# The second MLP's output product in seven block products, with its operand sums made by accumulating DMAs

## The chip, the cores and the metric

The kernel runs on one core of one Trainium2 chip. The metric is the device time of one execution in microseconds (us). The kernel before took 588.51 us (median of three runs, 586.87 to 592.11).

## The reference, cut to what matters

A sliding-window attention with sinks gives x (1536 tokens by 512), and two MLPs follow it:

```python
x = attention(q, k, v, n_sink, window)          # 1536 x 512
h = x @ w_in;   x = (h * clip(h + 3, 0, 6) / 6) @ w_out     # MLP1, d_ff = 2048
h = x @ w_in2;  g = h * sigmoid(1.702 * h)                  # MLP2, d_ff = 2048
out = g @ w_out2                                            # 1536 x 512, float32
```

Everything is float32. The change touches the last line alone, and of it two of the three blocks of 512 tokens.

## The kernel before, in words

**Products.** A float32 operand is split into a high part hi (rounded to the type fp32r) and the remainder lo, and a product a·b is three matmuls into one PSUM bank: hi·hi, hi·lo, lo·hi. A matmul loads 128x128 weights (LDWEIGHTS, row PEld of the profile) and streams 512 columns past them. The split of a 512-column tile is one cast on ACT (ScalarE) and one subtraction on DVE (VectorE).

**Stages.** The attention (24 steps) is interleaved with MLP1, whose three token blocks take 16 slices of d_ff (f) each: `up` (line 739, matmuls at L752) and `down` (L780, matmuls at L812). Then comes MLP2. Its middle token block runs alone, slice by slice, up and down. The first and the last block run together in the *pair* stage: for two slices of W_in at a time, `pair` (L585) takes the four quarters of that piece of W_in and of the two token blocks as a 2x2 block matrix product and computes it with seven block products instead of eight (Winograd's form of Strassen's method). Each block product is six matmuls at L628 into one of three banks p, q and s; the products b11, b21, t3, t2, t1, b22, t4 accumulate on those banks in turn, and between two products on the same bank ACT or DVE copies or adds what the bank holds so far (`put`, `add`). The sums of W_in's quarters are made by one DMA copy on the queue of SP, one accumulating DMA issued by POOL (L599) and three DVE instructions.

The gate then gives four quarters of g: two for the first token block, which are split and multiplied by W_out at once (24 matmuls at L812 per pair), and two for the last block, which are kept in spare tiles (`store`). When the eight pairs are through, the *rest* stage (`rest`, L729) multiplies the kept ones by W_out: 16 slices of 12 matmuls at L812, the last two slices quarter by quarter (`last_two`, L790) so that the results leave one after another. So W_out's product takes 2 x 16 x 12 = 384 matmuls of 512 columns for these two blocks.

**What sets the order.** The kernel runs under a hand-made planner (`Plan.issue`, L369). Each step is an `op` with the engines that may run it, a cost in ns, and a due time; `issue` plays the whole program with these costs, picks for the engine that can start soonest the step with the earliest due time, and emits the instructions in that order. On the chip each engine runs its own list in order and waits on semaphores; the DMAs that POOL issues stand in POOL's list, those of SP in SP's. Rings of buffers (`plan.ring`: w0, s, w1, g for split operands, u, aside and spare for float32 tiles, bank for the eight PSUM banks) bound how far a step may run ahead.

## Time and profile before

| what | value |
|---|---|
| runs | 588.51 us median of 3, 586.87 to 592.11 |
| profiled execution | 590.02 us, its span 587.9 us |
| TensorE (PE) busy | 569.3 us, 97% of the span |
| weight loads (PEld) | 492.8 us, beside the matmuls |
| DVE / ACT busy | 435.5 us (74%) / 365.0 us (62%) |
| POOL busy | 8.5 us |
| mean granted TensorE clock | 0.994 of full speed |

The span leaves out what lies before the first and after the last instruction, here 2.1 us. Busy times of PE overlap from one matmul to the next, since the end of a matmul is modelled: the distance from start to start tells how long one takes in a stream. The chain of waits follows the end of the program back from releaser to releaser. A duration on ACT or DVE is likewise longer than the distance to the next instruction on that engine.

### The profile page before, as it was taken

The numbers are of one execution on the slowest core, as the hardware profiler recorded it, in microseconds if no ns is written. First come the engines' busy times: TensorE is split into PE (matmuls) and PEld (weight loads), VectorE is DVE, ScalarE is ACT, GpSimd is POOL, SyncE is SP. The second block draws the span as 40 slices with busy tenths as digits, with TensorE's granted clock in tenths as the row PEclk, the third lists the DMA queues.
The fourth block names the chain that finished last, engine by engine and source line by source line (L and its number), as shares of the span: only waits on it lengthen the run. The fifth ranks groups of instructions, "written<-read, shape, count | busy, mean of one in ns | idle before, by whom it ended". The sixth has DMA issues, their size and how long they took to land.

```text
span 587.9 us, 10650 instructions
## 1 busy us (share of the span) xinstructions
PE 569.3 (97%) x4194; PEld 492.8 (84%) x4194; DVE 435.5 (74%) x912; ACT 365.0 (62%) x751; POOL 8.5 (1%) x18
## 2 busy tenths in 40 slices
PE   7789999999999999999999999999999999999996
PEld 6678877788888888888888888888888888888885
DVE  7799999999995756469999999973455555444542
ACT  6887775974666755465566596544575666455543
POOL 0000000000000000000000000000000100000000
PEclk8999999999999999999999999999999999999999
DMA  8974355145350000001444430510031110001102
GB/s 264 372 232 162 118 196 163 42 148 183 124 205 17 1 2 1 1 0 45 170 144 159 169 120 3 198 32 1 0 90 27 26 20 20 0 1 33 40 1 76
DMA packets 13480, 53.02 MB, mean 90 GB/s; under 512 B 1712, under 2 KB 3760, under 8 KB 9328
## 3 DMA queue, kind: packets, MB, share of 16 engines
q1 hardware_dynamic: 12272, 51.22, 26.0%
q0 software_dynamic: 1152, 1.05, 1.2%
q8 instruction: 35, 0.57, 0.4%
q14 instruction: 21, 0.17, 0.1%
HBM read 47.02 MB, written 3.15 MB: 85 GB/s over the span
## 4 chain that ended last, share of the span: by engine, by line
PE 76%; DVE 8%; ACT 7%; DMA 7%; issue 2%; SPq 0%; ACTq 0%
PE bank L812 37%; PE bank L752 22%; PE bank L628 12%; DMA stage<-in_w_dram 6%; ACT pexp L1011 3%; PE bank L1039 2%; PE bank L988 1%; DVE wf L503 1%; DVE wf L496 1%; ACT pexp L1028 1%; DMA wf<-in_kq_dram 1%; PE bank L1062 1%; ACT pts L445 1%; DVE pexp L1003 1%; ACT wf L475 1%
## 5 line engine op out<-in xcount | busy, mean ns | idle before, releaser
L812 PE MATMUL bank<-wg 128*128 128x512 f32 x1140 | 275.7, 381 | 0.5 <-ACT wg L445 0.3
L812 PEld LDWEIGHTS bank<-wg 128*128 128x128 f32 x1140 | 213.6, 189 | 32.6 <-DVE wg L570 1.3
L752 PE MATMUL bank<-xy,w0h 128*128 128x512 f32 x512 | 154.1, 382 | 1.5 <-DVE xy L1089 1.0
L752 PEld LDWEIGHTS bank<-xy,w0h 128*128 128x128 f32 x512 | 95.5, 189 | 15.3 <-DVE xy L1089 1.3
L752 PE MATMUL bank<-xy,w0l 128*128 128x512 f32 x256 | 97.0, 379 | 0.0
L554 DVE TENSOR_TENSOR wg<-wf,wg 128x512 fp32r<-128x512 f32 x95 | 65.3, 687 | 34.3 <-ACT wg L445 34.3
L445 ACT CAST wg<-wf 128x512 fp32r<-128x512 f32 x89 | 55.0, 618 | 44.7 <-PE bank L812 44.2
L570 DVE TENSOR_TENSOR wg<-u,wg 128x512 fp32r<-128x512 f32 x80 | 54.9, 687 | 13.8 <-ACT wg L445 12.9
L445 ACT CAST wg<-u 128x512 fp32r<-128x512 f32 x75 | 46.5, 620 | 19.7 <-DVE u L769 13.9
L554 DVE TENSOR_TENSOR w0l<-wf,w0h 128x512 fp32r<-128x512 f32 x72 | 49.3, 685 | 12.0 <-ACT w0h L445 11.8
L764 ACT ACTIVATE u<-bank,three 128x512 f32<-128x512 f32 x48 | 32.8, 684 | 40.1 <-PE bank L752 40.0
L752 PEld LDWEIGHTS bank<-xy,w0l 128*128 128x128 f32 x256 | 48.4, 189 | 6.8
L769 DVE SCALAR_TENSOR_TENSOR u<-u,bank 128x512 f32<-128x512 f32 x48 | 32.7, 682 | 25.9 <-ACT u L764 25.8
L1011 ACT ACTIVATE pexp<-pexp,nb 128x196 f32<-128x196 f32 x96 | 43.0, 450 | 8.6 <-DVE nb L1003 8.4
L475 ACT ACTIVATE wf<-stage 128x1024 f32<-128x1024 f32 x32 | 37.8, 1183 | 15.9 <-DMA stage<-in_w_dram 15.0
L445 ACT CAST w0h<-wf 128x512 fp32r<-128x512 f32 x60 | 36.7, 611 | 5.3 <-PE bank L628 4.6
L496 DVE SCALAR_TENSOR_TENSOR wf<-stage,wf 128x1024 int32<-128x1024 int32 x32 | 39.1, 1222 | 0.4
L503 DVE SCALAR_TENSOR_TENSOR wf<-stage,wf 128x1024 int32<-128x1024 int32 x32 | 39.1, 1221 | 0.2
L581 ACT ACTIVATE u<-bank 128x512 f32<-128x512 f32 x32 | 19.1, 596 | 31.1 <-PE bank L752 22.9
L628 PE MATMUL bank<-xy,w0h 128*128 128x512 f32 x128 | 38.1, 379 | 0.0
L1039 PE MATMUL bank<-ident,pexp 128*128 128x128 f32 x192 | 29.5, 296 | 4.1 <-DVE pexp L1030 2.3
L1039 PEld LDWEIGHTS bank<-ident,pexp 128*128 128x128 f32 x192 | 23.7, 151 | 9.3 <-ACT pexp L1028 2.3
(139 smaller groups left out, 630.4 us busy)
## 6 DMA issues: line engine op xcount, KB each, us to landing
stage<-in_w_dram SPq DMA_DIRECT2D x32, 1024.0 KB, 5.0
wf<-in_kq_dram SPq DMA_DIRECT2D x8, 520.0 KB, 11.1
vc<-in_vc_dram SPq DMA_DIRECT2D x12, 320.0 KB, 6.4
vb<-in_v_dram SPq DMA_DIRECT2D x10, 256.0 KB, 6.5
kept<-in_kq_dram SPq DMA_DIRECT2D x4, 520.0 KB, 10.9
out_dram<-stage SPq DMA_DIRECT2D x8, 256.0 KB, 3.0
aside<-wf SPq DMA_DIRECT2D x8, 128.0 KB, 2.0
aside<-wf POOLq DMA_DIRECT2D x8, 128.0 KB, 2.7
```

What stands on the lines that cost most here:

```text
L445: eng.copy(out, in_)
L475: lambda e: e.activation(w.tile.bitcast(F32), top.bitcast(F32), AF.Abs),
L496: lambda e: e.scalar_tensor_tensor(out=w.tile, in0=top, scalar=-0x40000000, in1=w.tile, op0=ALU.bitwise_and, op1=ALU.bitwise_or),
L503: lambda e: e.scalar_tensor_tensor(out=w.tile, in0=low, scalar=29, in1=w.tile, op0=ALU.logical_shift_right, op1=ALU.bitwise_or),
L554: lambda e: e.tensor_tensor(out=lo.tile[at], in0=of(), in1=hi.tile[at].bitcast(F32), op=ALU.subtract),
L570: lambda e: e.tensor_tensor(out=at(gl), in0=parted(u.tile), in1=at(gh).bitcast(F32), op=ALU.subtract),
L628: e.matmul(bank.tile, l, woven(r), start=(begin and j == 0 and k == 0), stop=(j == 1 and k == 2), skip_group_check=True,)
L752: e.matmul(h.tile[:, :n], w, woven(x), start=(c == 0 and k == 0), stop=(c == NC - 1 and k == 2))
L764: lambda e: e.activation(u.tile[:, :n], h.tile[:, :n], AF.Relu, bias=three, scale=1.0),
L812: e.matmul(yb.tile, l, woven(r), start=(begin and k == 0), stop=(end is not None and k == 2))
L1011: lambda e, n=n: e.activation(pes[n].tile[:, :W], pes[n].tile[:, :W], AF.Exp, bias=nbs[n].tile, scale=-1.0, accum_out=z.tile[:, n : n + 1],),
L1039: e.transpose(pt.tile[:, n * P : (n + 1) * P], pes[2 * a + j].tile[:, x * P : (x + 1) * P], ident)
```

## The change

W_out's product for the first and the last token block is now also a 2x2 block product in seven instead of eight: the rows are the two token blocks, the inner index the two slices of a pair (eight pairs), the columns the two halves of W_out's 512. A new function `downs` runs after all eight pairs and replaces `rest`, `last_two` and the 24 matmuls that each pair had. It computes seven products (numbered 0 to 6 below), each over eight pairs; each pair of a product is 12 matmuls of 256 columns (four 128-token quarters, three hi/lo parts). `left` splits a sum of g quarters, `right` a sum of W_out quarters; the signs go into the split. Sums are made in place by accumulating DMAs on POOL's queue (`more`): of W_out, 16 of 256 KB before product 2 and four more for product 3; of g, eight before the products, then eight in each of `after11`, `after12` and `after22`, beside products 0, 1 and 2. There are 52 in all. Two quarters of g now overwrite W_in's columns in their own tiles, two go negated by ACT into spare tiles. The mix of W_in that a DMA pair had made goes to DVE. The results of the two blocks leave in 16 stores of 128 KB. The planner counts 1300 ns of POOL for an issue; the accumulating DMAs' ring grows from 1 KB to 2 KB of each partition, and three mask tiles of together 1 KB become temporary. W_out's columns are laid out differently by the host, and the middle block's four results are put back in order by their copies.

```diff
@@ -425,6 +420,8 @@
                     self.dma_free = max(start + 600, self.dma_free) + cost
                     end = self.dma_free + LAND - 600
                     self.lanes.append(end + 300)
+                elif eng == "POOL":
+                    at[eng] = start + ISSUE
...
-            plan.op(
-                [("SP", 131072 / RATE_DMA)], lambda e: e.dma_start(out=s1(), in_=a21()), None, reads=[w2], writes=[sa],
-                chain="mix",
-            )
-            plan.op(
-                [("POOL", 3000)], lambda e: e.dma_start(out=s1(), in_=a22(), accum_op=ALU.add), None, reads=[w2],
-                writes=[sa], chain="mix",
-            )
             for to, x, y, how, reads, into in (
+                (s1, a21, a22, ALU.add, [w2], sa),
...
                 plan.op(
-                    [("PE", 6 * 216)], mm, due[i] + step[0] * 2037,
...
+                    [("PE", 6 * 216)], mm, due[i] + step[0] * 1296,
+                    reads=[wh, wl] + [b for x in xs for b in x[2]], writes=[bank], chain=("up", i),
...
-            u11, u21, one, low = Buf(cls="u"), Buf(cls="u"), Buf(cls="aside"), Buf(cls="aside")
-            g12, g22 = Buf(cls="spare"), Buf(cls="spare")
+            u11, u21, one, low = (Buf(cls="u") for _ in range(4))
+            n11, n12 = Buf(cls="spare"), Buf(cls="spare")
+            g21, g22 = (Buf(wf[f].bitcast(F32)[:, :512]) for f in (f1, f2))
...
             put(p, one, product(p, wa, 0, "b11", True))
             at = product(q, wa, 256, "b21", True)
             add(one, q, q, at)
             gate(q, u11, at + 600)
+            less(u11, n11, at + 1200)
+            put(p, low, product(p, wb, 256, "t2", False))
             put(s, g22, product(s, wb, 0, "t3", True))
-            at = product(p, wb, 256, "t2", False)
-            put(p, low, at)
-            g[i, 0] = split_g(u11, at)
-            wo[i, 0] = split_of(w1, slice(512, 1024), "w1", 1)
             at = product(p, wc, 0, "t1", False)
             add(g22, p, g22, at)
             gate(g22, g22, at + 1200)
-            at = product(p, wc, 256, "b22", False)
-            gate(p, g12, at)
             at = product(s, wd, 0, "t4", False)
             add(low, s, s, at)
             gate(s, u21, at + 600)
-            g[i, 1] = split_g(u21, at + 1200)
-            wo[i, 1] = split_of(w2, slice(512, 1024), "w1", 1)
-            store[f1], store[f2] = g12, g22
+            less(u21, n12, at + 1200)
+            gate(p, g21, product(p, wc, 256, "b22", False))
+            parts[f1 // 2] = {"11": n11, "12": n12, "21": g21, "22": g22}
+
+        def less(x, to, after):
+            plan.op([("ACT", 478)], lambda e: e.mul(to.tile, x.tile, -1.0), after, reads=[x], writes=[to])
+
+        def downs(t0):
...
+            for n in range(pairs // 2):
+                for k, (j, cols) in enumerate(((0, 0), (0, 256), (1, 0), (1, 256))):
+                    x = Buf(fa[:, 4 * n + j : 4 * n + 4 : 2, 512 + cols : 768 + cols])
...
+                less(b[n, "12"], b[n, "12"], None)
+                less(b[n, "21"], b[n, "21"], None)
+
+            def more(x, to):
+                plan.op(
+                    [("POOL", ADD_DMA)], lambda e: e.dma_start(out=to.tile, in_=x.tile, accum_op=ALU.add), None,
+                    reads=[x], writes=[to],
+                )
...
+            def left(x, sign, cls):
+                hi, lo = Buf(cls=cls + "h"), Buf(cls=cls + "l")
...
+                plan.op(
+                    [("ACT", 520)], lambda e: e.mul(at(hi), parted(x.tile), sign), None, reads=[x], writes=[hi],
+                    chain="split0",
...
+                plan.op(
+                    [("DVE", 602)],
+                    lambda e: e.scalar_tensor_tensor(
+                        out=at(lo), in0=parted(x.tile), scalar=sign, in1=at(hi).bitcast(F32),
+                        op0=ALU.mult, op1=ALU.subtract,
+                    ),
+                    None, reads=[x, hi], writes=[lo],
...
+            def right(x, cls="w1", to=None, after=()):
...
+                plan.op(
+                    [("ACT", 520)], lambda e: copy(e, at(hi), of()), None, reads=[x], writes=[hi], chain="split1",
...
+                plan.op(
+                    [("DVE", 602)],
+                    lambda e: e.tensor_tensor(out=at(lo), in0=of(), in1=at(hi).bitcast(F32), op=ALU.subtract),
...
+            def product(k, a, sign, r, bank, begin, then):
+                share = 4 // len(bank)
...
+                    def mm(e):
+                        at, gh, gl = x
+                        th, tl = (t.tile[:, :, n % 2 * P : (n % 2 + 1) * P] for t in y)
+                        for e4 in which:
+                            to = bank[e4 // share].tile[:, e4 % share * 256 : e4 % share * 256 + 256]
+                            hi, lo = quarter(at(gh), e4), quarter(at(gl), e4)
+                            for m, (l, t) in enumerate(((hi, th), (hi, tl), (lo, th))):
+                                e.matmul(
+                                    to, l, woven(t), start=(begin and n == 0 and m == 0 and e4 % share == 0),
+                                    stop=(n == pairs - 1 and m == 2), skip_group_check=True,
+                                )
...
+                    plan.op(
+                        [("PE", len(which) * 3 * 112)], mm, t0 + k * step + n * step // pairs,
...
+                w = []
+                for n in range(pairs):
+                    cls = ("w0", "s")[n % 2] if k < 2 else ("g", "w0", "s")[n % 3]
+                    if (k, n // 2) not in ready:
+                        ready[k, n // 2] = right(b[n // 2, r])
+                    w.append((left(parts[n][a], sign, cls), ready[k, n // 2]))
+                    then(n)
+                    if share == 2 or n < pairs - 2:
+                        quarters(n, *w[n], range(4))
+                if share == 1:
+                    for e4 in range(4):
+                        for n in range(pairs - 2, pairs):
+                            quarters(n, *w[n], [e4])
+                return t0 + (k + 1) * step
...
+            gone, ready = [x for half in halves(512, 512) for c in range(NC) for x in plan.x[half][c]], {}
+            for n in range(pairs // 2):
+                to = [Buf(home[1][:, :, n, :]) for home in (xyh, xyl)]
+                for x in to:
+                    x.readers = [o for y in gone for o in y.readers]
+                ready[0, n] = right(b[n, "11"], to=to)
+                more(b[n, "12"], b[n, "11"])
+            for n in range(pairs // 2):
+                ready[1, n] = right(b[n, "21"], "w1" if n < 2 else "g", None, [plan.last["g"]])
+                more(b[n, "11"], b[n, "21"])
+                more(b[n, "22"], b[n, "21"])
+                more(b[n, "22"], b[n, "12"])
+            bx, by, bz = ([Buf(cls="bank", kind="d") for _ in range(2)] for _ in range(3))
+            end = NBLK - 1
+            none = lambda n: None
+            for n in range(pairs):
+                more(parts[n]["22"], parts[n]["21"])
+
+            def after11(n):
+                more(parts[n]["21"], parts[n]["11"])
+
+            t1 = product(0, "11", -1.0, "11", bx, True, after11)
+            c11 = keep(bx, "u", 1.0, t1)
+
+            def after12(n):
+                more(parts[n]["11"], parts[n]["12"])
+                if n % 2 == 0:
+                    m = n // 2
+                    two = Buf(cls="aside")
+                    pairs_of = lambda: two.tile.rearrange("p (k n) -> p k n", k=2)
+                    plan.op(
+                        [("SP", 262144 / RATE_DMA)], lambda e: e.dma_start(out=pairs_of(), in_=b[m, "11"].tile), None,
+                        reads=[b[m, "11"]], writes=[two], after=[plan.last["mix"]],
+                    )
+                    plan.op(
+                        [("POOL", ADD_DMA)],
+                        lambda e: e.dma_start(out=pairs_of(), in_=b[m, "22"].tile, accum_op=ALU.add), None,
+                        reads=[b[m, "22"]], writes=[two],
+                    )
+                    b[m, "2"] = two
+
+            t2 = product(1, "12", 1.0, "21", by, True, after12)
+            add(by, c11, t2)
+            send(c11, 0, 0, t2)
+
+            def after22(n):
+                less(parts[n]["22"], parts[n]["22"], None)
+                more(parts[n]["11"], parts[n]["22"])
+
+            t4 = product(2, "22", -1.0, "21", bz, True, after22)
+            c22 = keep(bz, "u", -1.0, t4)
+            t6 = product(3, "11", 1.0, "2", bx, False, none)
+            c21 = keep(bx, "spare", 1.0, t6)
+            t7 = product(4, "22", -1.0, "12", bz, False, none)
+            add(bz, c21, t7)
+            send(c21, end, 0, t7)
+            t5 = product(5, "21", -1.0, "11", bx, False, none)
+            add(bx, c22, t5)
+            add(bz, c22, t5)
+            send(c22, end, 1, t5)
+            u4 = keep(bx, "spare", 1.0, t5)
+            bw = [Buf(cls="bank", kind="d") for _ in range(4)]
+            t3 = product(6, "12", -1.0, "22", bw, True, none)
...
+            for e4 in range(4):
+                plan.op(
+                    [("DVE", 335)],
+                    lambda e, e4=e4: e.tensor_tensor(
+                        out=c12[e4].tile[:, :256], in0=bw[e4].tile[:, :256],
+                        in1=u4[e4 // 2].tile[:, e4 % 2 * 256 : e4 % 2 * 256 + 256], op=ALU.add,
+                    ),
+                    t3, reads=[bw[e4], u4[e4 // 2]], writes=[c12[e4]],
+                )
+            send(c12, 0, 1, t3)
...
-        def rest(i):
-            which, t0, n, f, begin, end = items[i]
...
-        def last_two(i):
-
-            for e4 in range(4):
-                for k in (i - 1, i):
-                    which, t0, n, f, begin, end = items[k]
-                    down_of(g[k], wo[k], which, t0, n, begin, end, [due[k] + 1000] * 4, [e4])
...
+        if late:
+            downs(due[-1] + 9072)
...
                 if b.kind == "q":
-                    return h + used.count("q") < 4
+                    return h + used.count("q") < (4 if "y" in used else 6)
...
-                    t += {"pair": 14256, "rest": 2592}.get(items[n][0], 5184 * (RATE if n < 8 else RATE2 if n < 24 else 1))
+                    t += 9072 if items[n][0] == "pair" else 5184 * (RATE if n < 8 else RATE2 if n < 24 else 1)
...
-    nc = _bacc.Bacc("TRN2", target_bir_lowering=False, num_devices=1, dynamic_dma_scratch_size=1024)
+    nc = _bacc.Bacc("TRN2", target_bir_lowering=False, num_devices=1, dynamic_dma_scratch_size=2048)
...
-        return w.reshape(-1, w.shape[1] // 2, 2).transpose(0, 2, 1).reshape(w.shape)
+        return w.reshape(-1, 2, w.shape[1] // 4, 2).transpose(0, 1, 3, 2).reshape(w.shape)
```

Up to the first product of the pair stage, PE's list is the same in both kernels.

PE, the second pair of the pair stage. Before: `bank_4677`, `bank_4703` and `bank_4691` are p, s and q of that pair, the rows at L812 the matmuls with W_out.

```order
L628 MATMUL bank_4703<-xt_4031,sh_4032 128x512 x2
L628 MATMUL bank_4703<-xt_4031,sl_4034 128x512
...
L628 MATMUL bank_4677<-xt_4031,sh_4032 128x512 x2
L628 MATMUL bank_4677<-xt_4031,sl_4034 128x512
...
L812 MATMUL bank_4725<-wg_206 128x512 x3
L812 MATMUL bank_4731<-wg_206 128x512 x3
L628 MATMUL bank_4677<-xy_85,w0h_4672 128x512 x2
L628 MATMUL bank_4677<-xy_85,w0l_4675 128x512
...
L812 MATMUL bank_4649<-wg_206 128x512 x3
L812 MATMUL bank_4654<-wg_206 128x512 x3
```

PE, the same place now: `bank_4625` is p, `bank_4690` s, and nothing but products of pairs is left.

```order
L616 MATMUL bank_4625<-xt_4013,sh_4014 128x512 x2
L616 MATMUL bank_4625<-xt_4013,sl_4016 128x512
...
L616 MATMUL bank_4690<-xt_4013,sh_4014 128x512 x2
L616 MATMUL bank_4690<-xt_4013,sl_4016 128x512
...
L616 MATMUL bank_4625<-xy_70,w0h_4673 128x512 x2
L616 MATMUL bank_4625<-xy_70,w0l_4686 128x512
...
L616 MATMUL bank_4690<-xt_4013,sh_4015 128x512 x2
L616 MATMUL bank_4690<-xt_4013,sl_4017 128x512
```

Between two products on one bank there is now one product on the other, six matmuls; before, it was six and nine for p at the places shown, and more for s.

PE, the beginning of `downs` and the end of the last pair, as it stands now; `bank_5245` and `bank_5246` hold product 0.

```order
L616 MATMUL bank_5053<-xy_70,w0h_5091 128x512 x2
L616 MATMUL bank_5053<-xy_70,w0l_5094 128x512
L732 MATMUL bank_5245<-xy_70,w0h_5229 128x256 x2
L732 MATMUL bank_5245<-xy_70,w0l_5232 128x256
...
L732 MATMUL bank_5246<-xy_70,w0h_5229 128x256 x2
L732 MATMUL bank_5246<-xy_70,w0l_5232 128x256
```

In all 672 matmuls of 256 columns stand at L732, and none of 512 columns after the last pair.

POOL, the accumulating DMAs of g's sums. Before, POOL's list held eight accumulating DMAs, one for each pair:

```order
L599 DMA aside_3970<-wf1_63 128x256
L599 DMA aside_4537<-wf3_65 128x256
L599 DMA aside_4642<-wf5_67 128x256
L599 DMA aside_4743<-wf7_69 128x256
L599 DMA aside_4841<-wf9_71 128x256
```

Now, from the first of `after11` on; `stage` and `vc`, `vb` are spare tiles, a row into `stage0_60<-wf_62` is of `after11`, one into `wf_62<-stage0_60` of `after22`:

```order
L824 DMA aside_5199<-wf_62 128x2x256
L680 DMA stage0_60<-wf_62 128x512
L680 DMA wf_62<-wf_62 128x2x256
...
L680 DMA vc1_67<-wf_62 128x512
L680 DMA stage0_60<-stage0_60 128x512
L680 DMA stage1_61<-stage0_60 128x512
...
L680 DMA vc2_68<-vb1_64 128x512
L680 DMA wf_62<-stage0_60 128x512 x2
L680 DMA wf_62<-stage1_61 128x512 x2
...
L680 DMA wf_62<-vc1_67 128x512
L680 DMA vc2_68<-vc1_67 128x512
```

From the first `stage0_60<-wf_62` to `wf_62<-vc1_67` there are 26, which run in this order.

## Rows read from the trace of the kernel before

**Rows 1.** The page: busy time of each engine, share of the span, instructions.
```profile
PE 569.3 (97%) x4194; PEld 492.8 (84%) x4194; DVE 435.5 (74%) x912; ACT 365.0 (62%) x751; POOL 8.5 (1%) x18
```

**Rows 2.** Windows from the middle block's end: engines' busy us, clock, DMA share, GB/s.
```profile
core 0: us, PE busy (x) PEld busy (x) DVE busy (x) ACT busy (x) POOL busy (x), PEclk, DMA share, GB/s
395.00:424.60 29.60, 29.60 (x139) 25.92 (x138) 11.20 (x19) 13.51 (x25) 0.00 (x0) 1.00 0.00 1
424.60:480.00 55.40, 55.40 (x258) 48.53 (x257) 32.19 (x60) 35.55 (x66) 3.57 (x5) 1.00 0.17 41
480.00:535.30 55.30, 55.30 (x258) 48.40 (x257) 26.46 (x45) 29.26 (x53) 1.65 (x2) 1.00 0.04 8
535.30:582.70 47.40, 47.40 (x220) 41.20 (x218) 22.69 (x35) 23.63 (x42) 0.00 (x0) 1.00 0.12 32
582.70:587.90 5.20, 0.03 (x1) 0.00 (x0) 0.42 (x1) 0.37 (x1) 0.00 (x0) 1.00 0.48 136
```

**Rows 3.** Chain of waits, 423 to 588: start us, us, what.
```profile
424.74 1.29 PE bank L628 x6
...
535.46 47.28 PE bank L812 x219
...
582.76 0.38 ACT vc L445
...
583.17 0.42 DVE vc L447
```

**Rows 4.** Timeline of PE at 67 us: start us, us, instruction, count.
```profile
67.83 1.93 PE L1039 MATMUL bank<-ident,pexp 128*128 128x128 f32 x16
```

**Rows 5.** One line's instructions, L1039: duration ns min/median/max.
```profile
L1039 PE MATMUL bank<-ident,pexp x192: 272/273/473, 10.9 to 207.3; 128*128 128x128 f32 x192
```

**Rows 6.** Timeline of PEld at 96.7 us, behind a pause of PE.
```profile
96.77 0.30 PEld L752 LDWEIGHTS bank<-xy,w0h 128*128 128x128 f32 x2
```

**Rows 7.** One line's instructions, L752: duration ns min/median/max.
```profile
L752 PEld LDWEIGHTS bank<-xy,w0l x256: 189/189/189, 43.9 to 422.2; 128*128 128x128 f32 x128
```

**Rows 8.** Timeline of ACT in the rest stage.
```profile
538.74 0.62 ACT L445 CAST wg<-wf 128x512 fp32r<-128x512 f32 x1 [0.77 <-PE bank L812]
539.26 0.62 ACT L445 CAST wg<-stage 128x512 fp32r<-128x512 f32 x1
539.78 0.58 ACT L445 COPY stage<-bank 128x512 f32<-128x512 f32 x1
...
543.85 0.59 ACT L445 COPY vc<-bank 128x512 f32<-128x512 f32 x1
544.33 0.63 ACT L445 CAST wg<-wf 128x512 fp32r<-128x512 f32 x1
```

**Rows 9.** Timeline of DVE at 361 to 368 us.
```profile
361.47 0.69 DVE L722 SCALAR_TENSOR_TENSOR xt<-vb,xt 128x512 fp32r<-128x512 f32 x1
362.07 0.68 DVE L722 SCALAR_TENSOR_TENSOR xt<-aside,xt 128x512 fp32r<-128x512 f32 x1
...
366.82 0.42 DVE L609 TENSOR_TENSOR aside<-wf,wf 128x256 f32<-128x256 f32 x1
367.15 0.69 DVE L488 TENSOR_SCALAR wf<-wf 128x1024 int32<-128x1024 int32 x1
```

**Rows 10.** Timeline of the first pair: a product's last matmul, the copy or addition behind it.
```profile
425.65 0.38 PE L628 MATMUL bank<-xy,w0l 128*128 128x512 f32 x1
...
426.07 0.59 ACT L445 COPY aside<-bank 128x512 f32<-128x512 f32 x1 [0.68 <-PE bank L628]
...
428.24 0.38 PE L628 MATMUL bank<-xy,w0l 128*128 128x512 f32 x1
...
428.73 0.70 DVE L646 TENSOR_TENSOR bank<-aside,bank 128x512 f32<-128x512 f32 x1 [1.40 <-PE bank L628]
```

**Rows 11.** One line's instructions, L599: the accumulating DMAs that POOL issues.
```profile
L599 POOL DMA_DIRECT2D aside<-wf x8: 862/868/1020, 350.4 to 493.0; - x8
...
DMA to landing us min/median/max: 2.6/2.7/2.8
```

**Rows 12.** The page: DMA queues (packets, MB, share of 16 engines' span), issues (KB, us to landing).
```profile
q0 software_dynamic: 1152, 1.05, 1.2%
...
out_dram<-stage SPq DMA_DIRECT2D x8, 256.0 KB, 3.0
aside<-wf SPq DMA_DIRECT2D x8, 128.0 KB, 2.0
```

More of the change, by code (lines that the diff above doesn't have):

```diff
@@ L528, in plan_mlps @@
             items += [("pair", 0, 512, f, f == 0, None) for f in range(0, NF, 2)]
-            items += [("rest", (NBLK - 1) * 512, 512, f, f == 0, "y" if f == NF - 1 else None) for f in range(NF)]
         due = item_due(items)
         g, wo, ys = {}, {}, {}
-        sums, sixth, extra, store = {}, {}, {}, {}
+        sums, sixth, extra, parts = {}, {}, {}, {}
         def split(i, part):
@@ L727, in scaled @@
             )
-        def rest(i):
-            which, t0, n, f, begin, end = items[i]
-            g[i] = split_g(store[f], None, cls="s" if f == NF - 1 else "g")
-            if f < NF - 1:
-                wo[i] = split(i, 1)
-            else:
-                for k, b in enumerate(extra["t2", 0]):
-                    b.later = lambda k=k: late()["x"](2 * k)
-                wo[i] = split_of(plan.wf[f], slice(512, 1024), None, 1, True, extra["t2", 0])
         def up(i):
@@ L781, in down, with down_of @@
             which, t0, n, f, begin, end = items[i]
[L782 to L797 removed]
+            if which != "pair":
+                down_of(g.pop(i), wo.pop(i), which, t0, n, begin, end, [due[i] + DOWN] * 4)
+        def down_of(gs, ws, which, t0, n, begin, end, at):
             (gh, gl), (wh, wl) = gs, ws
@@ L800, in down_of @@
                 ys["b"] = [Buf(cls="bank", kind="y") for _ in range(4)]
-            for e4 in parts:
+            for e4 in range(4):
                 yb = ys["b"][e4]
@@ L855, in result @@
                 o = Buf(cls="spare" if late else "u")
-                if which == "rest" and e4 == 3:
-                    for x, opt in enumerate(([("ACT", 300)], [("DVE", 335)])):
-                        cols = slice(256 * x, 256 * (x + 1))
-                        plan.op(
-                            opt, lambda e, cols=cols: copy(e, o.tile[:, cols], yb.tile[:, cols]),
-                            when, reads=[yb], adds=[o],
-                        )
-                else:
-                    plan.op(
-                        [("ACT", 478), ("DVE", 602)], lambda e: copy(e, o.tile, yb.tile), when, reads=[yb], writes=[o]
-                    )
+                plan.op(
+                    [("ACT", 478), ("DVE", 602)],
+                    lambda e: copy(
+                        e, o.tile.rearrange("p (h n a) -> p h n a", h=2, a=2),
+                        yb.tile.rearrange("p (a n h) -> p h n a", h=2, a=2),
+                    ),
+                    when, reads=[yb], writes=[o],
+                )
                 rows = out[t0 : t0 + 512, :].rearrange("(l q h) d -> q h l d", l=8, q=4)[e4]
@@ L883, in plan_mlps @@
                     plan_load_w(plan, w2, f + nst - NF, None)
-            {"pair": pair, "rest": rest}.get(items[i][0], up)(i)
-            if i and (i < len(items) - 1 or items[i][0] != "rest"):
+            (pair if items[i][0] == "pair" else up)(i)
+            if i:
                 down(i - 1)
```

110 lines of the change are left out of this document (75 added, 35 removed).

## The prediction, as it was made before the changed kernel ran

> **What bounds the kernel now.** I read the busy times first: PE is busy for 97% of the span [rows 1]. That share alone could hide waits, so I went to windows by stage. From 395 us to 582.7 us PE is busy for all of every window, at a granted clock of 1.00, the 2.4 GHz level, while DVE and ACT are busy for 38% to 64% [rows 2]. The chain of waits says the same: from 424.74 us, where the pair stage begins, it runs over PE to 582.74 us, then through 0.38 us of ACT, 0.42 us of DVE and a store [rows 3]. So in the part that the change touches, time is the number of matmuls times the distance between two of them. That distance is 47.28/219 = 0.2159 us for 512 columns [rows 3]. The stage holds 336 matmuls of pair products and 384 with W_out, with 12 left of the middle block: 732 x 0.2159 = 158.0 us, and the chain has 582.74 - 424.74 = 158.0 us. Nothing else is in it.
>
> **The change, part by part.** The order of instructions ahead of the pair stage is the same, so nothing is won or lost there. The pair products keep their number and width.
>
> *Matmuls with W_out.* 384 matmuls of 512 columns go, 384 x 0.2159 = 82.9 us. In come 7 products x 8 pairs x 12 = 672 matmuls of 256 columns. No matmul of this width and type is in the trace. Half the columns cannot take less than half of 0.2159, 0.108 us, and should not take more than the whole 0.2159; in the same stream lies one weight load per matmul, so the question is whether a load of 128x128 fits into half the time. The nearest row: 16 transposes, each with its own 128x128 float32 load, take 1.93 us together; without the 0.27 us of the last one [rows 5] that is 1.66/15 = 0.110 us from start to start [rows 4]. For the type used here, two loads behind a pause of PE end 0.30 us after the first began; one lasts 0.189 us [rows 7], so the second began 0.11 us after the first [rows 6]. Both rows say that loads can follow at 0.11 us. I take 0.110: 672 x 0.110 = 73.9 us, a gain of **9.0 us** (10.3 at 0.108; at 0.2159 a loss of 62.2).
>
> The Trainium skill has a rule that speaks against this (TensorE: Matmul & The Clock Gate, Part 3, "The mechanism"): a weight load overlaps a running matmul only if it goes to another row group. All matmuls here use all 128 rows. The 512-column stream disagrees with it: load and stream would not fit into 0.2159 us one behind the other. It is a rival below.
>
> *ACT and DVE as possible bounds.* From start to start ACT takes 0.52 us for a cast and 0.48 for a copy from PSUM [rows 8], DVE 0.60 for 512 columns and 0.33 for 256 [rows 9]. In the new pair stage, 8 x 42 x 0.2159 = 72.5 us of PE, the changed order gives ACT 108 wide and 7 narrow instructions, at most 115 x 0.52 = 60 us, and DVE 52 wide and 35 narrow, 43 us. In `downs` ACT has 97, 50 us, DVE 85 wide and 4 narrow, 52 us, against 73.9 us. Neither becomes the bound by its total, and so the splits that the change adds (56 of g's sums, 28 of W_out's) cost nothing as long as they arrive in time. Without that cover each would cost the 0.52 + 0.60 us of its chain.
>
> *Turnarounds in the pair stage.* With the W_out matmuls gone, a bank is needed again after one other product, 6 x 0.2159 = 1.295 us. A copy by ACT ends at 426.66, that is 0.79 us after the last matmul gave way (425.65 + 0.216); an addition by DVE ends at 429.43, 0.97 us after 428.46 [rows 10]. So 0.50 and 0.33 us are left. Even in the old order one such gap of six matmuls, behind a copy, stood without a wait of PE [rows 2]. An instruction just begun on the engine holds the copy up by at most 0.52, the addition by 0.60 us. Of four turnarounds in each of eight pairs three go through ACT and one through DVE: 24 x 0.02 + 8 x 0.27 = 2.6 us if that always happens, 0 if never, 24 x 0.54 + 8 x 0.87 = 19.9 us if two instructions stand ahead each time. I take **1.5 us**, since DVE is busy about 60% of the time and mostly with one. In `downs` each pair's operands go ACT, DVE, PE, with four to six buffers; I take **1 us** for the change-over between stages (0 to 9: one pair's 12 x 0.110 = 1.3 us at each of seven products).
>
> *The end.* Before, ACT and DVE copied the two halves of the last bank one after the other; now one DVE addition of 256 columns follows the last matmul, so 0.4 us go [rows 3]. The last store is 128 KB, not 256. From 583.59 us to the span's end the old one took 4.3 us; a landing is 3.0 us for 256 KB to DRAM and 2.0 for 128 KB within the chip's memory [rows 12], so it gains between 0 and 1.0; I take 0.4. Together **0.8 us** (0.4 to 1.4).
>
> *POOL's sums.* The eight old accumulating DMAs took 0.87 us of POOL to issue and landed after 2.7 us [rows 11]; they moved 128 KB each, and 1.2% of 16 x 587.9 us over 8 is 14.1 us of one engine, 0.88 us of all sixteen [rows 12]. The new ones move 256 KB: between 0.88 us, were it all cost per packet, and 1.76 us, were it all bytes. The W_out sums have the 72.5 us of the pair stage. Product 3 reads g's sums of `after11`, product 4 those of `after22`, so 26 DMAs may run from the first split of product 0 (about 1 us before it starts) until product 4 wants its last pair (4 x 10.56 + 7 x 1.32 = 51.5 us after that start, less 1.5 us for the split). With 2.7 us for the last to land they stay hidden up to 48.3/26 = 1.86 us each. The upper end, 1.76, just fits: I charge nothing, and what is late if it does not fit is product 4. The larger ring and the moved mask tiles are charged nothing: POOL sends at most one DMA per 0.87 us, and the masks are made in the first microseconds, which the lists leave as they were. The strided copies of the middle block's four results run beside matmuls.
>
> *Sum*, against the profiled execution of 590.02 us: -9.0 + 1.5 + 1.0 - 0.8 = -7.3, 582.7 us. That execution lay 1.5 us above the median of the runs, so for the median **581.2 us**.
>
> **Rivals.**
> *The gain stays, but PE waits for copies and splits* in most turnarounds: 4 to 11 us of waits in place of 2.5. For it: the cover of 24 matmuls per pair is gone and the lists are fixed in advance. Against it: the loads of ACT and DVE. Time 582.7 to 589.7.
> *The sums of g come late* and product 4 waits: slower than before. The place is POOL's list from the first `stage<-wf` on, the price 26 x (r - 1.86) us for r us per DMA; it eats the whole gain at r = 2.14 and makes the kernel 1% slower at 2.37. At r = 2.5 it costs 16.6 us: 598 us. For it: the upper bound of r lies close to 1.86, and no row shows such DMAs back to back. Against it: fewer, larger packets cost less per byte. The Trainium skill's line for such DMAs (DMA: Bandwidth & Descriptors, "Anatomy of one DMA"), 2.0 us and bytes/436e3, would add an estimated 0.6 us for 256 KB each and keep them hidden; the trace's 2.7 us for 128 KB is above its 2.3.
> *Loads and matmuls run in turn*, 0.11 + 0.110 us each: 672 x 0.22 = 147.8 us, 73.9 more, 655 us. Against it stand [rows 3, 4].
> That the change does not do what it says is excluded by the lists: 672 matmuls of 256 columns stand there.
>
> **How the numbers follow.** A measurement here tells about 1%, 5.9 us, from no change, so faster means below 582.6. The forecast (waits up to 3.9 us) gets 0.52, and 576.8 to 582.6 us: at the low end -10.3 - 1.4 without any wait. The waits rival gets 0.25, of which 0.01 by the runs' scatter still counts as faster; the late sums get 0.13, of which 0.04 within 1%; the loads in turn 0.04; 0.06 what I have not named, spread evenly. Faster 0.55, same 0.30, slower 0.15. The range 576.8 to 592 holds the forecast, the waits and the mild half of the late sums, 0.8.
>
> **What would show it.** 672 matmuls at 0.110 us from start to start, with loads beside them, show the main term; 0.2 would refute it. Waits of PE in the pair stage on ACT copies or DVE additions above 3 us in all show the first rival. POOL's DMAs in `downs` more than 1.9 us apart, and PE, ACT or DVE waiting for them in product 3 or 4, show the second. From the last matmul to the end there should be 4.4 us. I am wrong if the pair stage is longer than 76 us or `downs` longer than 77.

## The result, and the profile after

The changed kernel takes 582.45 us (median of six runs, 581.77 to 584.52) where the kernel before took 590.38 us on the same chip (median of six): a ratio of 0.9879, 95% interval 0.9845 to 0.9914, so 1.2% faster and more than the 1% that the prediction set as the bound. Forecast were 581.2 us and a gain of 7.3; measured is a gain of 7.9 (5.1 to 9.2).

The profiled execution of the change took 584.52 us, the slowest of the six, with a span of 582.6. The page's busy times, which answer to [rows 1]:

```profile
PE 563.2 (97%) x4482; PEld 496.6 (85%) x4482; DVE 456.8 (78%) x951; ACT 389.4 (67%) x803; POOL 54.2 (9%) x62
```

The chain of waits, start us, us, what, which answers to [rows 3]:

```profile
426.10 1.29 PE bank L616 x6
427.39 2.59 PE bank L980 x12
429.98 71.92 PE bank L616 x330
501.89 75.05 PE bank L732 x672
576.95 0.02 issue
576.97 0.42 DVE vb L855
```

The chain still lies on PE from the start of the pair stage to the last matmul. The pair stage takes 501.89 - 426.10 = 75.79 us; its 348 matmuls (12 of the middle block among them) at 0.2159 us are 75.13, so waits can be 0.66 us at most; the trace lists no wait of PE from here to the last matmul. `downs` takes 75.05 us for 672 matmuls, 0.1117 us each, with no piece of another engine between. Together 150.84 us in place of 158.0, a gain of 7.2. Windows of the two stages, columns as in [rows 2]:

```profile
426.10:501.90 75.80, 75.80 (x350) 65.37 (x350) 48.06 (x91) 61.73 (x121) 27.45 (x24) 1.00 0.61 107
501.90:577.00 75.10, 75.03 (x672) 74.84 (x671) 53.95 (x86) 51.21 (x93) 25.30 (x28) 1.00 0.72 127
```

In `downs` the weight loads (third column) are now as busy as PE, 74.84 of 75.10 us; in [rows 2] they were 41.20 of 47.40. ACT is busy for 61.73 and 51.21 us, DVE for 48.06 and 53.95: below PE in both, and 2 to 12% above the 60 and 50, 43 and 52 us worked out.

The end grew. From the last matmul's end, 576.94 us, to the span's end, 582.6, are 5.65 us; before it was 587.9 - 582.74 = 5.16. In the two profiles the pair stage also begins 1.36 us later (426.10 after 424.74); with 0.2 us less outside the span this makes up the 5.5 us between them: 7.2 - 0.5 - 1.4 + 0.2.

### The profile page after: what moved, and what is told of

Read it like the earlier page. It is cut to its first block, busy times and chain, and to the rows that moved or that the text cites. A ratio compares the mean times of both kernels' runs of the same rounds, so it can differ in the third digit from the quotient of the medians.

```text
span 582.6 us, 11436 instructions
## 1 busy us (share of the span) xinstructions
PE 563.2 (97%) x4482; PEld 496.6 (85%) x4482; DVE 456.8 (78%) x951; ACT 389.4 (67%) x803; POOL 54.2 (9%) x62
## 3 DMA queue, kind: packets, MB, share of 16 engines
q0 software_dynamic: 10048, 13.63, 14.8%
## 4 chain that ended last, share of the span: by engine, by line
PE 80%; DVE 9%; ACT 4%; DMA 3%; issue 1%; DVEq 0%; SPq 0%
PE bank L980 24%; PE bank L932 24%; PE bank L732 13%; PE bank L616 13%; DMA stage<-in_w_dram 3%; PE bank L1203 2%; ACT pexp L1175 2%; PE bank L1152 2%; PE bank L1226 2%; DVE wf L500 1%; DVE wf L493 1%; PE bank L1234 1%; DVE pexp L1167 1%; DVE wg L550 1%; DVE wf L485 1%
## 5 line engine op out<-in xcount | busy, mean ns | idle before, releaser
L980 PE MATMUL bank<-wg 128*128 128x512 f32 x768 | 190.0, 382 | 2.7 <-ACT wg L442 2.5
L980 PEld LDWEIGHTS bank<-wg 128*128 128x128 f32 x768 | 143.3, 189 | 24.7 <-ACT wg L442 3.2
L680 POOL DMA_DIRECT2D wf<-wf x24 | 29.0, 1287 | 469.2 <-ACT wf L661 433.9
L442 ACT CAST wg<-wf 128x512 fp32r<-128x512 f32 x78 | 48.2, 618 | 31.9 <-PE bank L980 24.4
L550 DVE TENSOR_TENSOR wg<-wf,wg 128x512 fp32r<-128x512 f32 x64 | 43.9, 685 | 15.3 <-ACT wg L442 15.3
L442 ACT CAST wg<-u 128x512 fp32r<-128x512 f32 x59 | 36.6, 620 | 14.3 <-DVE u L949 14.3
L565 DVE TENSOR_TENSOR wg<-u,wg 128x512 fp32r<-128x512 f32 x64 | 43.9, 685 | 0.9
## 6 DMA issues: line engine op xcount, KB each, us to landing
wf<-in_kq_dram SPq DMA_DIRECT2D x8, 520.0 KB, 11.8
```

What stands on the lines that cost most here:

```text
L442: eng.copy(out, in_)
L550: lambda e: e.tensor_tensor(out=lo.tile[at], in0=of(), in1=hi.tile[at].bitcast(F32), op=ALU.subtract),
L565: lambda e: e.tensor_tensor(out=gl.tile, in0=parted(u.tile), in1=gh.tile.bitcast(F32), op=ALU.subtract),
L980: e.matmul(yb.tile, l, woven(r), start=(begin and k == 0), stop=(end is not None and k == 2))
```

## Experiments

Each ratio is against the kernel before on the same chip. The difference to the changed kernel is (ratio / 0.9879 - 1) x 582.45 us; with both intervals it is known to 3 or 4 us. e2, e12 and e6 leave out part of the sums and serve for times alone.

| run | median, us | ratio, 95% interval | to the change, us |
|---|---|---|---|
| e1_halves (of before) | 593.56 | 1.0057, 1.0032 to 1.0082 | |
| e2_narrow | 583.83 | 0.9884, 0.9830 to 0.9937 | +0.3 |
| e12_narrow2 | 580.72 | 0.9842, 0.9800 to 0.9884 | -2.2 |
| e3_oldchain | 592.51 | 1.0050, 1.0027 to 1.0073 | +10.1 |
| e10_chain | 582.01 | 0.9874, 0.9841 to 0.9907 | -0.3 |
| e6_nosums | 583.42 | 0.9869, 0.9832 to 0.9907 | -0.6 |
| e4_dma8 | 593.87 | 1.0079, 1.0053 to 1.0105 | +11.8 |
| e5_dma8b | 587.33 | 0.9959, 0.9931 to 0.9986 | +4.7 |
| e8_ring1k | 601.32 | 1.0155, 1.0098 to 1.0211 | +16.3 |
| e9_late | 595.72 | 1.0112, 1.0064 to 1.0160 | +13.7 |
| e11_noissue | 593.63 | 1.0081, 1.0039 to 1.0122 | +11.9 |
| e7_tail | 582.50 | 0.9858, 0.9823 to 0.9893 | -1.2 |

### What a matmul of 256 columns costs

**e1_halves.** The kernel before, W_out's matmuls of the two blocks in halves:

```diff
-e.matmul(yb.tile, l, woven(r), ...)
+for j in range(2):    # pair and rest stage
+    e.matmul(yb.tile[:, j * 256 : (j + 1) * 256], l, woven(r[:, :, j * P : (j + 1) * P]), ...)
```

> The kernel before, with each of the 384 matmuls with W_out of the first and the last token block done as two of 256 columns (768 in place of 384); nothing else is changed. If a 256-column matmul always costs the 0.1117 us of the changed kernel's stream (75.05/672): 768 x 0.1117 = 85.8 us for 82.9, so +2.9 us. If 0.110, the prediction's value, were right and the rest of the 75.05 us were small waits: +1.6 us. If half the columns cost half the time (0.108): 0. If the weight loads cost more where the operands lie otherwise: above +5 us.

It is slower by 0.57%, 3.4 us (1.9 to 4.8), where 2.9 were expected. The chain's last long piece, in the rest stage of this run:

```profile
535.75 48.92 PE bank L815 x438
```

48.92/438 = 0.1117 us: the cost goes with the width, in the old place and order too, and is no wait of `downs`.

**e2_narrow, e12_narrow2.** Product 5 streams half the columns; the second run also halves its weights' columns:

```diff
-to, l, woven(t), ...
+to[:, : 2 * few], l, woven(t[:, :, :few]), ...             # e2: few = 64 for product 5, else 128
+to[:few, : 2 * few], l[:, :few], woven(t[:, :, :few]), ...  # e12
```

> The changed kernel, with product 5 streaming 128 of each 256 columns (half of that product's sums are left out). If the weight load sets the 0.1117 us, the distance stays at 0.11 and product 5 takes its 10.7 us as before: the time of the changed kernel, 582.5 us. If the columns set it (256/2.4 GHz and 5 ns), the distance falls to 0.058 inside a group of 12 matmuls, and product 5 shrinks until ACT (16 casts of 0.52 us) or DVE (16 of 0.60 us) bounds it at about 8.3 to 9.6 us: 1 to 2.5 us less.

> As the run with 128 columns streamed in product 5, and with weights of 64 columns in place of 128 there (three quarters of that product's sums are left out). If the load's time goes with the weights' columns, the distance between matmuls falls to about 0.06 us; if it goes with the rows (128, as before) or is fixed, it stays at 0.11 us.

The chain of e2, and then PE's timeline of e12 (start us, us, instruction, count) around the beginning of product 5:

```profile
503.59 75.05 PE bank L733 x672
```

```profile
555.64 0.86 PE L733 MATMUL bank<-wg 128*64 128x128 f32 x12
556.34 0.28 PE L733 MATMUL bank<-wg,w0h 128*64 128x128 f32 x2
```

In e2, 672 matmuls take 75.05 us to the hundredth, though 96 of them stream half as many columns. In e12 twelve follow at (556.34 - 555.64)/12 = 0.058 us. So the 0.1117 us is the time of a load of 128 weight columns, and the stream of 256 columns is hidden beside it; a load of 64 columns takes at most 0.058. The Trainium skill (TensorE: Matmul & The Clock Gate, "LDWEIGHTS (loading the stationary operand)") says that a load goes with the weights' columns, about columns/1.2 in ns, an estimated 107 ns for 128. The runs agree to 5%, with 111.7.

### What hides the turnarounds

**e3_oldchain, e10_chain.** Both give the pairs one chain; e3 also takes back the order of the block products.

```diff
-reads=[wh, wl] + [b for x in xs for b in x[2]], writes=[bank], chain=("up", i),
+reads=[wh, wl] + [b for x in xs for b in x[2]], writes=[bank], chain="up",
...
-            put(p, low, product(p, wb, 256, "t2", False))    # from here e3 alone
             put(s, g22, product(s, wb, 0, "t3", True))
+            put(p, low, product(p, wb, 256, "t2", False))
...
+            gate(p, g21, product(p, wc, 256, "b22", False))
             at = product(s, wd, 0, "t4", False)
...
-            gate(p, g21, product(p, wc, 256, "b22", False))
```

> The changed kernel with the block products of a pair in the order of the kernel before and with one chain for all pairs, so that t2, t1 and b22 stand on one bank one behind the other with nothing between in the last five pairs. If the turnaround is what the prediction took it for (copy 0.79 us, addition 0.97 us behind the last matmul), PE waits 5 x (0.8 + 1.0) = 9 us more: about 591.5 us. If ACT and DVE come later or earlier than that in the list (the waits go to the splits), 0 to 4 us more. If it is the load on ACT and DVE and not the order that makes waits, no change.

> The changed kernel with its new order of block products, but one chain for all pairs, so that in the last five pairs each turnaround of a bank has exactly one other product (1.30 us) beside it. If the turnarounds' 0.79 us (ACT) and 0.97 us (DVE) fit with what stands ahead on these engines: under 1 us more, 582 to 584 us. If an instruction just begun there usually holds them up: 5 pairs x 4 x up to 0.3 us = up to 6 us more.

e3 costs 10.1 us, e10 nothing. PE's waits in e3 from 425 us on (engine, line, what it waited for: us in total, times, longest):

```profile
PE bank L616 <- ACT u L442: 4.4, 5, 0.9
PE bank L616 <- DVE wf L634: 3.9, 5, 0.8
```

Five pairs, one copy and one addition each, 8.3 us: the turnaround is 0.8 to 0.9 us of wait where no other product stands beside it, and e10, whose trace has no wait of PE there, shows that one product of 1.30 us covers it. The separate chains per pair are not needed for that; the order of the products is.

### What hides the sums

**e6_nosums.** `more` does nothing. That leaves out 48 of the 52 accumulating DMAs (the 44 of 48 in the expectation were miscounted).

```diff
             def more(x, to):
+                return
```

> The changed kernel without 44 of the 48 accumulating DMAs outside the pair pieces (all sums that are made in place, of W_out and of g, are left out; the four that build product 3's right operand stay); PE, ACT, DVE and SP have the same instructions in the same order. If the sums are hidden, as the prediction charged them: no change, 582.5 us, +-1. If they cost something through the DMA engines or memory ports that the waits do not show (slower casts, slower matmuls, the issue of the last stores): 1 to 4 us faster.

No difference that can be told, and the chain has 75.05 us for 672 matmuls again. The sums cost nothing as they are.

**e4_dma8, e5_dma8b.** Eight more, spread through the sums of g:

```diff
             def after12(n):
+                plan.op([("POOL", ADD_DMA)], lambda e: e.dma_start(
+                    out=(xyh, xyl)[n // 4][0][:, :, n % 4, :].bitcast(F32),
+                    in_=parted(parts[n]["22"].tile),    # e4
+                    in_=b[n // 2, "22"].tile,           # e5
+                    accum_op=ALU.add), t0, ...)
                 more(parts[n]["11"], parts[n]["12"])
```

> The changed kernel with eight more accumulating DMAs of 256 KB on POOL's queue, into dead tiles (nothing reads them), spread through the sums of g. If the DMA engines are the limit there (about 1.7 us each, so 26 sums stay 26 x 0.16 = 4 us inside the limit of 1.86), the last sums land 13.6 us later and PE waits 13.6 - 4 = 9 to 10 us in product 4: about 592 us. If it is the latency of each and not the throughput that counts, or if the sums are far from being late: no change, under 1 us.

> As the run with eight more accumulating DMAs, but they read quarters of W_out that nothing writes afterwards, so that no instruction of ACT has to wait for them; only the DMA engines and POOL's list are lengthened. If the engines' throughput is the limit (1.7 us each): the sums land up to 13.6 us later, 4 us of it inside the limit, and PE waits 5 to 10 us in products 3 and 4: 588 to 593 us. If the 11 us of the run before came from ACT's negations waiting for the added reads alone: 582 to 584 us.

e4 met its 592 us for a reason of its own: ACT negates parts 22 in place, had to wait for the added reads, and held up the casts behind it. In e4's waits:

```profile
ACT wf L661 <- DMA xy<-wf: 10.0, 2, 5.9
PE bank L732 <- ACT wg L442: 8.6, 1, 8.6
```

The kernel loses more than this wait: behind it, from 542.2 to 546.2 us, the granted clock is 0.50 (more on this at e8).

e5 removes that and costs 4.7 us, just under the 5 to 10 expected. POOL's timeline, first in the changed kernel (the first of 27 DMAs from the first sum of `after11` on, nearly all of them sums of g; the last that product 4 reads; the last of all, which product 6 reads), then the same two of e5:

```profile
502.78 1.40 POOL L680 DMA_DIRECT2D stage<-wf  x1
...
537.94 0.86 POOL L680 DMA_DIRECT2D wf<-vc  x1 [0.85 <-ACT wg L442]
539.22 0.86 POOL L680 DMA_DIRECT2D vc<-vc  x1 [0.42 <-POOLq L1430]
```

```profile
541.60 0.86 POOL L680 DMA_DIRECT2D wf<-vc  x1 [0.51 <-issue]
...
549.24 0.86 POOL L680 DMA_DIRECT2D vc<-vc  x1 [0.42 <-POOLq L1438]
```

In the changed kernel the issues are (539.22 - 502.78)/26 = 1.40 us apart. The page's DMA rows show what that leaves out (KB each, median us from issue to landing; the queue's packets, MB, share of 16 engines):

```profile
vc<-vc POOLq DMA_DIRECT2D x1, 256.0 KB, 10.2
q0 software_dynamic: 10048, 13.63, 14.8%
```

The last sum lands 10.2 us after its issue, at 549.4, the first 5.2 us after its own, at 508.0: they land (549.4 - 508.0)/26 = 1.59 us apart. And 14.8% of 16 x 582.6 us over 52 DMAs is 1.66 us of all engines each. The window from the first issue to the last landing (columns as in [rows 2]) has the DMA engines as good as full, with a mean share of 1.03; one cast already waits 0.5 us for a sum (ACT's waits), without PE coming to a stop:

```profile
502.80:549.40 46.60, 46.60 (x419) 46.60 (x419) 31.73 (x50) 34.81 (x65) 24.54 (x28) 1.00 1.03 175
```

```profile
ACT wg L690 <- DMA wf<-vb: 0.5, 1, 0.5
```

In e5 the last issue comes 10.0 us later, but POOL's order has changed as well, and the last sum for product 4 is issued only 3.7 us later. The chain of e5 shows where PE pays, at the fifth pair of product 4, behind such a sum (672 - 239 = 433 matmuls are done there, and product 4 begins with the 385th):

```profile
538.70 9.01 DMA wf<-vb
...
551.98 26.97 PE bank L732 x239
```

In this trace `downs` takes 3.4 us longer than 75.05. Whether the engines or the ring (below) held the eight added DMAs up was not separated.

**e8_ring1k.** The ring of before:

```diff
-dynamic_dma_scratch_size=2048)
+dynamic_dma_scratch_size=1024)
```

> The changed kernel with the accumulating DMAs' ring of 1 KB of each partition, as before the change, in place of 2 KB; the instruction lists are the same. If the ring is not what POOL waits for: no change, 582.5 us. If it is (256 descriptors for each 256 KB, POOL's issues of 2.1 to 2.6 us in the trace lengthen and fewer DMAs are under way): the sums come 1.9 to 2.5 us apart, product 4 waits, 584 to 598 us.

16.3 us slower than the change and 1.6% slower than before, with the same instructions. POOL's timeline at the sums of W_out:

```profile
493.14 1.22 POOL L824 DMA_DIRECT2D aside<-wf  x1 [3.25 <-issue]
497.25 1.21 POOL L680 DMA_DIRECT2D wf<-wf  x1 [2.89 <-PE bank L616]
501.34 1.22 POOL L824 DMA_DIRECT2D aside<-wf  x1 [2.88 <-DVE sl L695]
505.61 1.21 POOL L824 DMA_DIRECT2D aside<-wf  x1 [3.05 <-issue]
...
519.57 1.43 POOL L680 DMA_DIRECT2D stage<-wf  x1
```

These DMAs, whose rows are cut in two pieces of 1 KB, go one by one, 4.1 us apart, each 2.9 us of pause after an issue of 1.2; the releasers named differ from row to row while the pause does not. The times to landing of those into `aside` say what the pause is:

```profile
DMA to landing us min/median/max: 3.8/3.8/4.0
```

Each starts about 0.3 us after the one before has landed. In the changed kernel several are under way at once:

```profile
487.84 2.12 POOL L680 DMA_DIRECT2D wf<-wf  x2 [2.75 <-ACT wf L576]
489.13 2.08 POOL L824 DMA_DIRECT2D aside<-wf  x1
490.90 1.55 POOL L680 DMA_DIRECT2D wf<-wf  x1
493.35 1.20 POOL L824 DMA_DIRECT2D aside<-wf  x1 [0.89 <-DVE w0l L550]
496.81 1.20 POOL L824 DMA_DIRECT2D aside<-wf  x1 [2.27 <-DVE wf L634]
```

The one of 489.13 landed 7.4 us after its issue, at 496.5. Two more were issued before that, and the third 0.3 us behind it: three at once.

So in e8 the first sum of g (`stage<-wf`) comes at 519.57 instead of 502.78, 16.8 us late. That this is about the loss is chance. In e8's trace `downs` takes 93.27 us, 18.2 more than 75.05, in two parts. PE waits 11.3 us, 11.1 of them in two waits for casts; the chain shows a late sum ahead of the second:

```profile
PE bank L732 <- ACT wg L442: 11.1, 2, 7.5
```

```profile
554.01 4.22 DMA wf<-stage
...
560.27 34.76 PE bank L732 x287
```

Behind each of the two waits the granted clock is 0.50, the 1.2 GHz level (windows, columns as in [rows 2]):

```profile
535.60:541.20 5.60, 5.60 (x26) 5.60 (x27) 3.01 (x5) 3.03 (x6) 3.06 (x4) 0.50 1.03 174
560.30:565.20 4.90, 4.90 (x23) 4.90 (x24) 2.98 (x5) 2.76 (x6) 2.20 (x3) 0.50 1.03 175
```

Some 49 matmuls take 10.5 us here, 0.214 each, where at 1.00 they would take 49 x 0.1117 = 5.5: another 5 us. The remaining 1.9 us were not traced.

**e9_late.** The sums of W_out stand behind the first pairs' sums of g in POOL's list:

```diff
-more(b[n, "12"], b[n, "11"])
+more(b[n, "12"], b[n, "11"], [last])    # and so for all 16
```

> The changed kernel with the 16 in-place sums of W_out not made ahead: in POOL's list they stand behind the sums of g of the first six pairs or later, so that they are issued from about 501 us on, when the pair stage ends; PE, ACT, DVE and SP have the same lists. If the DMA engines' throughput is what counts (1.7 us each), 44 sums then have the 52 us until product 4 wants its last pair, room for 30: 14 x 1.7 = 24 us late, 600 to 612 us. If there is room (below 1.2 us each): 582 to 585 us.

13.7 us slower: the direction expected, but below the 17.5 to 29.5 us. Of its 52 DMAs 47 are issued from 488.21 to 558.71, (558.71 - 488.21)/46 = 1.53 us apart; they began 13 us earlier than the expectation had it. They do take the 1.7 us each that it counted: the first landed at 491.7, the last at 568.2, 76.5/46 = 1.66 us apart. The last sum is issued 19.5 us later than in the change. PE waits 5.6 us, and behind its longest wait the clock is 0.50 here too, from 549.6 to 555.0 us:

```profile
PE bank L732 <- ACT wg L442: 4.7, 2, 2.8
```

**e11_noissue.** The planner counts POOL as busy until a sum lands:

```diff
-                elif eng == "POOL":
-                    at[eng] = start + ISSUE
```

> The changed kernel with the planner counting POOL as busy for a sum's whole 4500 ns in place of 1300 ns for its issue; this moves four to eight sums of W_out behind sums of g in POOL's list and leaves PE's list as it is. If the order of the sums has slack (the last waits in the trace are 0.5 us): 582 to 585 us. If the sums of W_out then come late for product 4, 585 to 595 us.

11.9 us slower, with PE's list unchanged; in its trace `downs` takes 84.7 us, 9.7 more than in the change. The cause is not the one expected: PE waits for casts and copies, and the chain of waits in `downs` runs over PE, ACT and DVE and never over a DMA. PE's waits:

```profile
PE bank L730 <- ACT wg L688: 3.0, 3, 1.2
PE bank L730 <- ACT stage L760: 1.6, 1, 1.6
PE bank L730 <- ACT w0h L688: 1.2, 1, 1.2
PE bank L730 <- DVE wg L693: 0.9, 3, 0.3
```

These are 6.7 of the 9.7 us. The count changes the order of ACT's and DVE's lists as well. ACT's waits in `downs` for a buffer that PE still reads, ahead of casts of W_out, first of the change, then of e11:

```profile
ACT wg L442 <- PE bank L732: 9.1, 12, 1.5
```

```profile
ACT wg L440 <- PE bank L730: 16.7, 14, 2.1
```

Behind these waits stand, in ACT's list, casts that PE needs next. That the changed order is the cause was not tried by a run of its own, and the other 3 us were not traced.

### The end

**e7_tail.** The second and fourth of the last four stores go by ACT:

```diff
-[("SP", 131072 / RATE_DMA)],
+[("ACT", 60)] if share == 1 and e4 % 2 else [("SP", 131072 / RATE_DMA)],
```

> The changed kernel with the second and the fourth of the last four stores issued by ACT in place of SP. In the changed kernel's trace the last result is ready at 577.39 us and its store begins at 578.2, behind the store before it on SP. If that queue is the cause: the last store begins within 0.1 us of its result, and from the last matmul to the end it takes 4.9 us in place of 5.65, about 581.7 us (within what a measurement can tell). If the issue is slow for another reason (the DMA rings, the stores' small pieces): 5.6 us as before.

The queue's timeline (SPq, ACTq: the engines' issues), first of the change, then of e7:

```profile
576.08 1.40 SPq L781 DMA_DIRECT2D out_dram<-vc  x1
577.58 1.22 SPq L781 DMA_DIRECT2D out_dram<-vb  x2
```

```profile
575.98 0.54 SPq L781 DMA_DIRECT2D out_dram<-vb  x1
576.65 0.56 ACTq L781 DMA_DIRECT2D out_dram<-vb  x1
```

In the change the issue of the second store takes 1.40 us and the last one starts at 578.2, 0.8 us after its result. In e7 it starts at once, but the last matmul ends at 576.17 and the span at 581.8: 5.6 us as before. The last store takes 5.1 us from its issue there, 4.4 in the change. SP's queue was a delay, but not what set the end: the last store's landing did. Times to landing, for the last two stores of the change (min/median/max; 3.4 is the last one's), then for the last store of e7 (the page's DMA rows):

```profile
DMA to landing us min/median/max: 2.4/2.9/3.4
```

```profile
out_dram<-vb ACTq DMA_DIRECT2D x1, 128.0 KB, 4.1
```

The span ends 1.0 us after that landing in both. Why the last store takes 4.1 us when it starts earlier was not tried.

## Why the prediction was right

**The main term: right in kind, 15% too large.** 384 x 0.2159 = 82.9 us became 672 x 0.1117 = 75.05, a gain of 7.85, not 9.0. Part of it is rounding: the rows give 1.66/15 = 0.1107 and 0.111, not 0.110, which makes the gain 8.3. They were rows of loads one behind the other, and that is what binds: e2 shows that the load alone sets the distance. With that read as the bound and not as a check, the columns' 0.108 would have dropped out as an end of the range.

**Turnarounds: mis-sized.** At most 0.66 us, not 1.5; the change-overs in `downs` 0, not 1. The bounds of 0.02 and 0.27 per turnaround took every copy to find its engine busy; e10 shows that one product beside it is enough, e3 that nothing beside it costs 0.8 to 0.9 each, which the 0.79 and 0.97 us of [rows 10] gave.

**The end: wrong.** It grew by 0.5 us instead of falling by 0.8. The step from two copies to one addition happened (0.42 us from 576.97), but the last store did not start behind its result, and a smaller store did not land sooner: 3.4 us (4.1 in e7) against 3.0 for the 256 KB of before, and 4.4 and 5.1 us from its issue to the end, against the 4.3 that the prediction read.

With the right sizes the sum is -7.85 + 0.66 + 0.5 = -6.7 us for these parts; the errors of the forecast (1.15 us too much gained, 1.8 too much charged, 1.3 at the end) nearly cancelled. That 7.3 us came so close to the measured 7.9 is luck in part.

**Ahead of the pair stage** no change was forecast. In nine traces with the change's list of PE there (the change, e2, e4 to e9, e12) the stage begins at 424.6 to 427.8 us, in two with the old one (before, e1) at 424.7 and 423.8. The nine alone differ by 3.2 us, e4 and e5, which differ in what a DMA of `downs` reads, by 2.9; so the 1.36 us between the two profiles cannot be told from scatter.

**POOL's sums: the number held, and one reason did not.** That they are hidden is shown by e6; that the margin is small, by e5. The prediction put the limit at 1.86 us each and the sums at 0.88 to 1.76. They landed 1.59 us apart, with issues 1.40 apart and so a growing queue: 10.2 us from issue to landing at the end, not 2.7. The last sum for product 4 landed at 537.94 + 10.2 = 548.1; its last pair is due at 501.89 + 39 x 1.34 = 554.2, less 1.5 for the split, 552.7, so 4.6 us were left there. But "The larger ring and the moved mask tiles are charged nothing: POOL sends at most one DMA per 0.87 us" was wrong in its reason. POOL is also held by what the ring can take: with the old ring it sends one per 4.1 us of the strided kind (rows in two pieces) and the whole gain is gone (e8). That the sums of W_out are made ahead of time (e9) and the planner's count (e11) carry as much. Each was a cover to be priced, at 12 to 16 us: the ring and the early sums are two more ways into the rival "the sums of g come late", the count is one into late casts. And the rival's price, 26 x (r - 1.86), holds the wait alone: behind long waits PE also ran at the 1.2 GHz level, which cost 5 us more in e8.

**The other rivals.** Loads and matmuls in turn, 0.22 us, is refuted by e2: a stream of 128 or 256 columns hides wholly beside the load. The Trainium skill's rule (TensorE: Matmul & The Clock Gate, Part 3, "The mechanism") that a load overlaps only with a matmul of another row group does not hold in these streams, whose loads all use 128 rows (the same section also names a background weight buffer). Waits for copies and splits did not come.

None of the versions tried beats the changed kernel by more than the measurement can tell (e10 and e7 are within their intervals); the rest are slower or leave work out.

## What to carry to other kernels

Price a matmul by the larger of its stream and its weight load: at half the width a block product with seven of eight matmuls keeps 75.05/82.9 = 0.905 of the time, not 0.875. A transfer that is off the path needs three things priced apart from its bytes: how many its ring lets run at once, where it stands in its queue, and what the order of the other engines assumes of it. Read its rate from landings, not from issues. And a long wait of TensorE can cost more than its length, since the clock may be lower behind it.

## What was not expected of the hardware

An accumulating DMA of 256 KB whose rows are two pieces of 1 KB held POOL 1.2 us and, with a ring of 1 KB per partition, kept the next one of its kind back until 0.3 us after it had landed, 4.1 us after its own start; with 2 KB three were under way. In `downs`, with the DMA engines as good as full (1.03), the last one (rows in one piece) landed 10.2 us after its issue, while the 24 of `wf<-wf`, most of them in the pair stage, had a median of 3.9. Behind waits of PE of 2.8 to 8.6 us (e9, e8, e4) the granted clock stood at 0.50, and a matmul of 256 columns took 0.214 us in place of 0.1117. A store's issue on SP took 0.54 us, but 1.40 for the second of the last four, and 1.31 and 1.20 for the same one in e2 and e6.
